# Memory attention and a four-expert feed-forward: the product of v_m and w1, by pairs of batches or by fours through device memory

## The chip, the cores and the metric

The kernel runs on one core of one Trainium2 chip. The metric is the device time of one execution in microseconds (us); three timed executions of the kernel before gave 1426.92, 1427.36 and 1427.86 us, median 1427.36 us. A separate execution was profiled.

## What is computed

An attention over 32 memory slots for each of 8 batches and 8 heads, and then a feed-forward of four experts over all 4608 rows. Cut to what matters:

```
a = softmax(phi, axis=2)                                   # (8, 8, 576, 32)
k_m = einsum('bhsm,bhsd->bhmd', a, k)
v_m = einsum('bhsm,bhsd->bhmd', a, v)                      # (8, 8, 32, 64)
attn = softmax(q @ k_m^T / 8)                              # (8, 8, 576, 32)
x = (attn @ v_m) laid out as (4608, 512)
for e in range(4):
    h = relu(x @ w1[e])                                    # (4608, 1024)
    out += p[:, e:e+1] * (h @ w2[e])
```

The kernel doesn't form x. It multiplies v_m of a batch with w1 first (256 rows, 8 heads of 32 slots, by 1024), and the attention weights with that product: h = relu(attn @ (v_m w1)).

## The kernel before

All values are fp32, and each large product is made as three TensorE matmuls on split operands: a value is held as a high part (a cast to fp32r) and a low part (value minus high part), and high*high, high*low and low*high are added in PSUM. ScalarE (ACT) makes the high part, VectorE (DVE) the low one.

The eight batches are worked through in four pairs (`k`), and in each pair the four experts (`e`). One pair and expert is a block of 32 steps: 16 for the even batch, 16 for the odd one (`odd`), each in two halves of 8 steps (`j`, one slice of 128 of the 1024 hidden columns). There are 512 steps. In a step, `first` (L415 to L417) multiplies attention weights `AT` with the product `vw` for the step after next (`AHEAD = 2`); ACT and DVE make `h` (and `hm`) of it (L427, L429); `second` (L445 to L447) multiplies `h` of this step with `w2` into PSUM, and after 8 steps DVE adds the result to `acc` (L460, L462).

Everything else is spread over the steps by tables: `plan` holds for each step the units that are written into the program ahead of the step's own matmuls. In each block:

- `unit_w2` (steps 20 to 27) and `unit_w1` (steps 24 to 30) split the next block's weights (ACT L118, DVE L119) from a staged load (`stage`, 512 KB each, five buffers, issued in order by SyncE, SP).
- `vw_unit` (steps 26 to 33) makes the next block's product of v_m and w1: for each half of w1 and each pair of heads three matmuls (L364 to L366, stationary `vt`, moving `w1`) into a tile `pv`. The stationary operand `vt` holds both batches of the pair, two heads of each on the diagonal, so one `pv` serves both; ACT and DVE split it into the two batches' `vw` tiles, 64 partitions at a time (L379, L380).
- The attention of the next pair's batches (softmax of phi, `unit_kv`, `kv_pick`, `write_vt`, scores and transposes) has step tables of its own (`UNITS_EVEN`, `UNITS_ODD`).

A scheduler then fixes each engine's order, with the place in the program as priority; each engine runs its queue in that order. Ahead of step 0 stands a part whose order is written by hand: batch 0's attention, its first products and the first two `first`. There `kv_pick` (L261, L265) and `write_vt` (L291) feed the scores and the first `pv`, and the chain reduce, add, reciprocal, multiply (L326 to L329) gives the attention weights, which PE transposes (L349) and DVE splits into `AT` (L356).

Of the kernel before, what the change touches and what calls it, by code (L numbers as in the profile page):

```python
# [68 lines left out]
def body(ctx: ExitStack, tc: tile.TileContext, qm, qt, kv, kvt, phi, prob, w1, w2, out):  # L70
    nc = tc.nc
    pool = lambda name, **k: ctx.enter_context(tc.tile_pool(name=name, bufs=1, **k))
    const, wp, work, att = pool("const"), pool("wp"), pool("work"), pool("att")
# [207 lines left out]
    def write_vt(b, a=slice(0, 2)):  # L281
        k, odd = b // 2, b % 2
        if ("vt", k) not in st:
            st["vt", k] = att.tile([P, NP, 2, P], F32R, name="vt", tag="vt", bufs=2)
        vt = st["vt", k].rearrange("p (a two) h c -> p a two h c", two=2)
        v = kvT[odd].rearrange("p w (a two) c -> p w a two c", two=2)
        for par in range(2):
            dst = vt[:, a, par ^ odd, :, 64 * par:64 * par + 64]
            src = v[:, 1, a, par, :]
            nc.scalar.copy(dst[:, :, 0, :], src)  # L290
            nc.vector.tensor_sub(dst[:, :, 1, :], src, dst[:, :, 0, :].bitcast(F32))  # L291
# [77 lines left out]
    def vw_out(ps, fh, hp, odds):  # L369
        g = hp // 2  # L370
        for odd in odds:
            if hp % 2 == 0:
                vw[odd, fh, g] = att.tile(
                    [P, 2, 512], F32R, name="vw", tag=f"vw{odd}", bufs=4 + odd
                )
            q = (hp % 2) ^ odd
            r = slice(64 * q, 64 * q + 64)
            t = vw[odd, fh, g]
# [289 lines left out]
```

## Time and profile before

| | before |
|---|---|
| median of three executions | 1427.36 us |
| profiled execution | 1428.84 us, of it span 1427.1 us |
| PE (TensorE) busy | 1412.3 us, 99% |
| DVE busy | 837.2 us, 59% |
| ACT busy | 620.2 us, 43% |
| loads and stores | 113.86 MB, 24.5% of the 16 DMA engines' span |

The span reaches from the first to the last instruction of the program; the profiled execution's own time is 1.74 us longer. A matmul's record is longer than its pitch, since matmuls are pipelined: one of 512 columns has a record of 0.39 us. What one costs where PE is never idle is therefore read from the starts of neighbours in the timeline, not from the mean of a group.

### The profile page before, as it was taken

Reading aid. Unit: us, or ns where it says so; the run is one execution under the profiler, and the core shown is the slowest. Engines: PE = TensorE matmul, PEld = TensorE weight load, DVE = VectorE, ACT = ScalarE, POOL = GpSimd, SP = SyncE. Lnnn points to the kernel's source line nnn. Section 1 sums busy time; section 2 is a strip of 40 time slices with the busy share of each in tenths; the row PEclk is TensorE's granted clock in tenths of the full one; section 3 lists DMA queues with packets and bytes.
Section 4 is the critical chain, followed back from the end, with each engine's and each line's share of the span. In section 5 each row is a group of like instructions: output and inputs, shape, how many; then the busy total and the mean of one; then the engine's idle time right before and its main releaser. Section 6 shows DMA issues by size and latency. Waiting matters only on the chain.

```text
span 1427.1 us, 20830 instructions
## 1 busy us (share of the span) xinstructions
PE 1412.3 (99%) x7808; PEld 1233.5 (86%) x7808; DVE 837.2 (59%) x1853; ACT 620.2 (43%) x1543; POOL 27.8 (2%) x27
## 2 busy tenths in 40 slices
PE   7999999999999999999999999999999999999998
PEld 6888888888888888888888888888888888888887
DVE  7876638666385654837547375573846446272722
ACT  6655426453263533635335362452625234161521
POOL 3300000000000000000000000000000000000000
PEclk8999999999999999999999999999999999999999
DMA  6632303323141120412214121140323103030001
GB/s 245 198 118 75 121 28 126 104 64 104 39 161 61 64 89 16 137 58 78 94 63 135 59 88 65 46 130 18 107 75 96 60 25 94 1 119 1 1 30 38
DMA packets 35957, 115.20 MB, mean 81 GB/s; under 512 B 3984, under 2 KB 5136, under 8 KB 35856
## 3 DMA queue, kind: packets, MB, share of 16 engines
q1 hardware_dynamic: 35856, 113.86, 24.5%
q8 instruction: 62, 1.02, 0.3%
q14 instruction: 39, 0.32, 0.1%
HBM read 104.41 MB, written 9.44 MB: 80 GB/s over the span
## 4 chain that ended last, share of the span: by engine, by line
PE 92%; DMA 2%; DVE 2%; ACT 2%; issue 1%; POOL 0%; SPq 0%; ACTq 0%
PE p L446 18%; PE p L447 18%; PE p L445 18%; PE p L415 9%; PE p L417 9%; PE p L416 9%; PE sc L304 2%; PE pv L366 2%; PE pv L364 2%; PE x L230 2%; PE pv L365 2%; DMA stage<-in_w 1%; PE tp L349 1%; PE kvp L249 1%; ACT w L118 0%
## 5 line engine op out<-in xcount | busy, mean ns | idle before, releaser
L446 PE MATMUL p<-w,h 128*128 128x512 f32 x1024 | 404.3, 395 | 0.0
L447 PE MATMUL p<-w,h 128*128 128x512 f32 x1024 | 402.8, 394 | 0.0
L445 PE MATMUL p<-w,h 128*128 128x512 f32 x1024 | 402.7, 393 | 0.0
L427 ACT ACTIVATE h<-p 128x256 fp32r<-128x256 f32 x512 | 195.2, 382 | 331.5 <-PE p L417 294.3
L429 DVE SCALAR_TENSOR_TENSOR h<-p,h 128x256 fp32r<-128x256 f32 x512 | 213.9, 418 | 206.3 <-ACT h L427 110.0
L415 PE MATMUL p<-AT,vw 128*128 128x256 f32 (+1 forms) x1024 | 308.2, 301 | 0.0
L417 PE MATMUL p<-AT,vw 128*128 128x256 f32 (+1 forms) x1024 | 304.3, 297 | 0.1
L416 PE MATMUL p<-AT,vw 128*128 128x256 f32 (+1 forms) x1024 | 303.6, 297 | 0.0
L447 PEld LDWEIGHTS p<-w,h 128*128 128x128 f32 x1024 | 192.4, 188 | 43.3 <-DVE nm L154 0.2
L119 DVE TENSOR_TENSOR w<-stage,w 128x512 fp32r<-128x512 f32 x259 | 175.9, 687 | 78.4 <-ACT w L118 77.1
L445 PEld LDWEIGHTS p<-w,h 128*128 128x128 f32 x1024 | 193.2, 189 | 23.3
L446 PEld LDWEIGHTS p<-w,h 128*128 128x128 f32 x1024 | 192.6, 188 | 22.0
L416 PEld LDWEIGHTS p<-AT,vw 128*128 128x128 f32 x1024 | 194.5, 190 | 19.5 <-DVE AT L356 0.3
L415 PEld LDWEIGHTS p<-AT,vw 128*128 128x128 f32 x1024 | 194.0, 189 | 19.1
L417 PEld LDWEIGHTS p<-AT,vw 128*128 128x128 f32 x1024 | 193.5, 189 | 0.7 <-DVE vw L380 0.6
L118 ACT CAST w<-stage 128x512 fp32r<-128x512 f32 x262 | 159.6, 620 | 79.1 <-DMA stage<-in_w 47.3
L380 DVE TENSOR_TENSOR vw<-pv,vw 64x512 fp32r<-64x512 f32 x254 | 172.1, 685 | 8.9 <-ACT vw L379 5.5
L429 DVE SCALAR_TENSOR_TENSOR hm<-p,hm 128x64 fp32r<-128x64 f32 x256 | 56.0, 219 | 201.9 <-ACT h L427 200.9
L379 ACT CAST vw<-pv 64x512 fp32r<-64x512 f32 x254 | 145.5, 580 | 58.5 <-DVE vw L380 42.6
L427 ACT ACTIVATE hm<-p 128x64 fp32r<-128x64 f32 x256 | 56.6, 221 | 227.9 <-PE p L417 227.9
L462 DVE SCALAR_TENSOR_TENSOR acc<-p,pt,acc 128x512 f32<-128x512 f32 x96 | 67.8, 741 | 2.6 <-PE p L447 2.6
L366 PE MATMUL pv<-w,vt 128*128 128x512 f32 x136 | 53.7, 395 | 0.0
(81 smaller groups left out, 1020.5 us busy)
## 6 DMA issues: line engine op xcount, KB each, us to landing
stage<-in_w SPq DMA_DIRECT2D x132, 512.0 KB, 3.8
stage<-in_kv SPq DMA_DIRECT2D x32, 512.0 KB, 4.1
stage<-in_qm SPq DMA_DIRECT2D x16, 512.0 KB, 3.7
out<-acc SPq DMA_DIRECT2D x32, 256.0 KB, 2.1
ph<-in_phi SPq DMA_DIRECT2D x16, 288.0 KB, 3.5
stage<-in_kvt SPq DMA_DIRECT2D x8, 512.0 KB, 3.8
stage<-in_qt SPq DMA_DIRECT2D x8, 128.0 KB, 3.2
out<-accm SPq DMA_DIRECT2D x4, 256.0 KB, 2.2
```

The source lines that it names most:

```text
L118: nc.scalar.copy(dst[:, 0, :], raw)
L119: eng.tensor_sub(dst[:, 1, :], raw, dst[:, 0, :].bitcast(F32))
L379: nc.scalar.copy(t[r, 0, :], ps[r])
L380: nc.vector.tensor_sub(t[r, 1, :], ps[r], t[r, 0, :].bitcast(F32))
L415: nc.tensor.matmul(ps, w[:, 0, f], at_t[:, g, 0, c], start=g == 0, stop=False)
L416: nc.tensor.matmul(ps, w[:, 0, f], at_t[:, g, 1, c], start=False, stop=False)
L417: nc.tensor.matmul(ps, w[:, 1, f], at_t[:, g, 0, c], start=False, stop=g == 1)
L427: nc.scalar.activation(t[:, 0, to], ps[:, at_], AF.Relu)
L429: nc.vector.scalar_tensor_tensor(t[:, 1, to], ps[:, at_], 0.0, t[:, 0, to].bitcast(F32), ALU.max, ALU.subtract)
L445: nc.tensor.matmul(po[t], x[:, 0, :], w[:, 0, :], start=j == 0, stop=False)
L446: nc.tensor.matmul(po[t], x[:, 0, :], w[:, 1, :], start=False, stop=False)
L447: nc.tensor.matmul(po[t], x[:, 1, :], w[:, 0, :], start=False, stop=j == NJ - 1)
```

## The change

- **Fours.** For some experts the product of v_m and w1 is made once for four batches (two pairs) and not once for each pair. `four` takes one head of w1 (64 rows, loaded twice into 128 partitions, input `w1d`), splits it, and multiplies with `vs`: 64 partitions of v's high part and 64 of its low part, four batches side by side in the 128 columns. Two matmuls give (high + low) * (w1 high + w1 low). `FOUR = (3, 0)`: batches 0 to 3 for expert 3 alone, batches 4 to 7 for all four experts. The other experts of batches 0 to 3 keep `vw_unit`.
- **Through device memory.** The 128x512 result is split into a tile `vst` of 128x2x512 (512 KB; ACT L466, DVE L467), which goes to device memory by one transfer (`to_memory`, L453), written in the program with the next `four`. For each block `load_vw` then loads a batch's rows: per batch and half of w1 eight transfers of 32 partitions, 128 KB each (L483), into the same `vw` tiles as before. All are issued by SP.
- **Where they stand.** In the blocks that make fours, one `four` a step in steps 8 to 23 (`FOUR_AT`), loads at steps 20, 25, 28 and 32 (`VW_LOAD_AT`); the blocks are the third of pair 0, the last of pair 1 and the first three of pair 2. Five other blocks (the third of pair 1, the last of pair 2, the first three of pair 3) have the loads alone, and no product of v_m and w1.
- **Attention.** Keys and values of batches 2 to 7 are made earlier, in tables of their own (`ATT`), since v of four batches must be there before the first `four`. The keys lie in four tiles `kT`, v apart in `v`. `kv_pick` has eight instructions for half as many elements each where it had four; `write_vs` and `v_hi` are added for every batch, `write_vt` stays for batches 0 to 3, in smaller pieces.
- **Buffers.** `stage` 5 to 4, `w2` 10 to 9, `kvs` (shared by `vst`) 2 to 3.

The diff, cut to its core:

```diff
-STAGE = 5
-KVS = 2
+STAGE = 4
+KVS = 3
 AHEAD = 2
+VW_LOAD_AT = ((20, 25), (28, 32))
+TURN = (0, 2, 1, 3)
+
+FOUR = (3, 0)
+
+FOUR_AT = ((8, 10, 12, 14), (16, 18, 20, 22))
...
-UNITS_EVEN = (0, 4, 6, 6, 7, 9, 10, 13, 16, 19, 22, 37, 42, 42, 46, 49, 49)
-UNITS_EVEN_0 = (29, 33, 36, 37, 37, 39, 40, 43, 46, 49, 50, 64, 69, 73, 73, 80, 81)
-UNITS_ODD = (63, 66, 68, 69, 69, 71, 72, 75, 78, 81, 84, 99, 104, 104, 109, 111, 112)
+
+
+PHI = 3
+KV_STEPS = (5, 5, 6, 8, 9, 12, 15, 18, 21)
+EVEN, ODD = (0, 4, 4, 8, 11, 11), (0, 5, 5, 10, 12, 13)
+ATT = {
+    2: (0, 27, (73, EVEN)), 3: (0, 49, (99, ODD)),
+    4: (PAIR, 2, (37, EVEN)), 5: (PAIR, 28, (99, ODD)),
+    6: (PAIR, 54, (PAIR + 37, EVEN)), 7: (PAIR, 80, (PAIR + 99, ODD)),
+}
...
-    kvT = [const.tile([P, 2, NP, 2 * M], F32, name=f"kvT{i}") for i in range(2)]
-    for t in kvT:
+    kT = [const.tile([P, NP, 2 * M], F32, name=f"kT{i}") for i in range(4)]
+    vts = [const.tile([P, NP, 2, P], F32R, name=f"vt{i}") for i in range(2)]
+    for t in [vts[0].bitcast(F32)] + kT + [vts[1].bitcast(F32)]:
         nc.gpsimd.memset(t, 0.0)
...
-                t = wp.tile([P, 2, DM], F32R, name="w2", tag="w2", bufs=NJ + 2)
+                t = wp.tile([P, 2, DM], F32R, name="w2", tag="w2", bufs=NJ + 1)
...
-        kvd = kvT[b % 2][:, :, 2 * g:2 * g + 2]
-        kvp = st["kvp", b, g].rearrange("p h w c -> p w h c")
-        for i in range(2):
-            r, m = slice(64 * i, 64 * i + 64), slice(M * i, M * i + M)
-            if i == 0:
-                nc.scalar.copy(kvd[r, :, :, m], kvp[r, :, :, m])
-            else:
-                nc.vector.tensor_copy(kvd[r, :, :, m], kvp[r, :, :, m])
-        for i in range(2):
-            r, m = slice(64 * i, 64 * i + 64), slice(M * i, M * i + M)
-            lo = slice(2 * M + M * i, 2 * M + M * i + M)
-            nc.vector.tensor_add(kvd[r, :, :, m], kvd[r, :, :, m], kvp[r, :, :, lo])
+        if g == 0:
+            st["v", b] = att.tile([P, NP, M], F32, name="v", tag="v", bufs=2)
+        for w in (1, 0):
+            for i in range(2):
+                r, m = slice(64 * i, 64 * i + 64), slice(M * i, M * i + M)
+                lo = slice(2 * M + M * i, 2 * M + M * i + M)
+                a = slice(2 * g, 2 * g + 2)
+                dst = st["v", b][r, a] if w else kT[b % 4][r, a, m]
+                src = st["kvp", b, g][r, :, w]
+                (nc.vector.tensor_copy if i else nc.scalar.copy)(dst, src[:, :, m])
+                nc.vector.tensor_add(dst, dst, src[:, :, lo])
...
+    def slot(b, h):
+        return h ^ TURN[b % 4]
+
+    def v_hi(b, gs=slice(0, 2)):
+
+        if ("vh", b) not in st:
+            st["vh", b] = att.tile([P, NP, M], F32R, name="vh", tag="vh")
+        split = lambda t: t.rearrange("p (g a) m -> p g a m", g=2)
+        v, vh = split(st["v", b]), split(st["vh", b])
+        if gs is not None:
+            nc.scalar.copy(vh[:, gs], v[:, gs])
+        return v, vh
+
+    def write_vt(b, gs=slice(0, 2)):
+
+        v, vh = v_hi(b, None)
+        vt = vts[b // 2].rearrange("p (g a) s c -> p g a s c", g=2)
+        for h in range(4):
+            q = slot(b, h)
+            r, rq = (slice(64 * (i % 2), 64 * (i % 2) + 64) for i in (h, q))
+            dst = vt[r, gs, h // 2, :, M * q:M * q + M]
+            x, hi = v[rq, gs, q // 2, :], vh[rq, gs, q // 2, :]
+            if r == rq:
+                nc.scalar.copy(dst[:, :, 0, :], x)
+                hi = dst[:, :, 0, :]
+            else:
+                nc.vector.tensor_copy(dst[:, :, 0, :], hi.bitcast(F32))
+            nc.vector.tensor_sub(dst[:, :, 1, :], x, hi.bitcast(F32))
+
+    def write_vs(b):
+
+        if b % 4 == 0:
+            st["vs", b // 4] = att.tile([P, 2, 4, P], F32R, name="vs", tag="vs")
+        vs, (v, vh) = st["vs", b // 4], v_hi(b, None)
+        for h in range(4):
+            q = slot(b, h)
+            rq, c = slice(64 * (q % 2), 64 * (q % 2) + 64), slice(M * q, M * q + M)
+            x, hi = v[rq, :, q // 2, :], vh[rq, :, q // 2, :]
+            if q % 2 == 0:
+                nc.scalar.copy(vs[:64, :, h, c], hi.bitcast(F32))
+            else:
+                nc.vector.tensor_copy(vs[:64, :, h, c], hi.bitcast(F32))
+            nc.vector.tensor_sub(vs[64:, :, h, c], x, hi.bitcast(F32))
...
+    vwd, done = {}, []
+
+    def to_memory():
+        for key, t in done:
+            vwd[key] = dram.tile([P, 2, 512], F32, name="vwd" + "".join(map(str, key)))
+            nc.sync.dma_start(vwd[key], t.bitcast(F32))
+        done.clear()
+
+    def four(n, e, fh, h, raw):
+
+        to_memory()
+        g, vs = h // 4, st["vs", n]
+        w = wp.tile([P, 2, 512], F32R, name="w1", tag="w1", bufs=4)
+        split(w, raw[:, h % 2, :], nc.vector)
+        ps = psum.tile([P, 512], F32, name="pv", tag="pm", bufs=4)
+        for a in range(2):
+            nc.tensor.matmul(ps, vs[:, g, h % 4, :], w[:, a, :], start=a == 0, stop=a == 1)
+        t = att.tile([P, 2, 512], F32R, name="vst", tag="kvs", bufs=KVS)
+        nc.scalar.copy(t[:, 0, :], ps)
+        nc.vector.tensor_sub(t[:, 1, :], ps, t[:, 0, :].bitcast(F32))
+        done.append(((n, e, fh, g, h % 4), t))
+
+    def units_four(n, e, fh, hp):
+        kept = []
+        def emit(raw):
+            kept.append(raw)
+            four(n, e, fh, 2 * hp, raw)
+        return (("w1d", e, fh, hp), emit), lambda: four(n, e, fh, 2 * hp + 1, kept[0])
+
+    def load_vw(k, e, odd, fh):
+        b = 2 * k + odd
+        for g in range(2):
+            t = vw_tile(k, e, odd, fh, g)
+            for h in range(4):
+                r = slice(M * slot(b, h), M * slot(b, h) + M)
+                nc.sync.dma_start(t[r].bitcast(F32), vwd[b // 4, e, fh, g, h][r])
...
+        def write():
+            v_hi(b)
+            if b < 4:
+                write_vt(b)
+            write_vs(b)
+        u += [write]
...
+                by_four = ne >= FOUR[nk // 2]
                 n = 0
                 for fh in range(2):
-                    for g in range(2):
+                    for hp in range(NP if by_four and nk % 2 == 0 else 0):
+                        for i, u in enumerate(units_four(nk // 2, ne, fh, hp)):
+                            at(s + FOUR_AT[fh][hp] + i, u)
+                    if by_four and nk % 2 == 0:
+                        at(s + FOUR_AT[fh][NP - 1] + 2, to_memory)
+                    for odd in range(2 if by_four else 0):
+                        at(s + VW_LOAD_AT[odd][fh], lambda a=(nk, ne, odd, fh): load_vw(*a))
+                    for g in range(0 if by_four else 2):
                         at(s + W1_AT[2 * fh + g], unit_w1(nk, ne, fh, g))
...
-        if k + 1 < NG:
-            b = 2 * k + 2
-            for bb, U in ((b, UNITS_EVEN_0 if k == 0 else UNITS_EVEN), (b + 1, UNITS_ODD)):
-                s0 = k * PAIR
-                at(s0 + U[0], lambda bb=bb: load_phi(bb))
-                at(s0 + U[1], lambda bb=bb: phi_chain(bb))
-                for n, u in enumerate(att_units(bb)):
-                    at(s0 + U[2 + n], u)
+    for b in range(2, B):
+        s0, kv_at, sc_at = ATT[b]
+        u = att_units(b)
+        at(s0 + kv_at, lambda b=b: load_phi(b))
+        at(s0 + kv_at + PHI, lambda b=b: phi_chain(b))
+        for d, x in zip(KV_STEPS, u[:9]):
+            at(s0 + kv_at + d, x)
+        for d, x in zip(sc_at[1], u[9:]):
+            at(s0 + sc_at[0] + d, x)
...
-        write_vt(1)
...
+    v_hi(0)
+    write_vs(0)
...
+        "w1d": c(
+            np.tile(moe_w1.reshape(E, NP, 2, D, 2, 512).transpose(0, 4, 1, 3, 2, 5), (1, 1, 1, 2, 1, 1))
+        ),
```

On PE, a step in the last eight of a block before (one `vw_unit`), and a step of a block with fours after; `vt` and `vs` are the stationary operands with v, `w` is split w1. Before:

```order
L447 MATMUL p_7353<-w_6546,h 128x512
L364 MATMUL pv<-w_7459,vt 128x512
L365 MATMUL pv<-w_7459,vt 128x512
L366 MATMUL pv<-w_7459,vt 128x512
L415 MATMUL p_7523<-AT,vw 128x256
```

After:

```order
L537 MATMUL p_8399<-w_7895,h 128x512
L464 MATMUL pv<-w_8437,vs 128x512 x2
L505 MATMUL p_8446<-AT,vw 128x320
L506 MATMUL p_8446<-AT,vw 128x320
L507 MATMUL p_8446<-AT,vw 128x320
```

Where three matmuls of 512 columns stood between two steps' own, two stand. In the whole program the first form goes from 136 units (408 matmuls) to 56 (168), and 80 of the second (160 matmuls) are new.

On DVE, in the part ahead of step 0, between the sum of the first softmax and the first split of `AT`. Before:

```order
L327 TENSOR_SCALAR z<-z 128x16
L328 RECIPROCAL z<-z 128x16
L329 TENSOR_TENSOR at<-at,z 128x512
L380 TENSOR_TENSOR vw<-pv,vw 64x512
L119 TENSOR_TENSOR w_420<-stage,w_420 128x512
L356 TENSOR_TENSOR AT<-tp,AT 128x2x256
```

After:

```order
L341 TENSOR_TENSOR vs<-v,vh 64x2x32
L377 TENSOR_SCALAR z<-z 128x16
L340 CAST vs<-vh 64x2x32
L341 TENSOR_TENSOR vs<-v,vh 64x2x32
L378 RECIPROCAL z<-z 128x16
L341 TENSOR_TENSOR vs<-v,vh 64x2x32
L379 TENSOR_TENSOR at<-at,z 128x512
L340 CAST vs<-vh 64x2x32
L435 TENSOR_TENSOR vw<-pv,vw 64x512
L341 TENSOR_TENSOR vs<-v,vh 64x2x32
L138 TENSOR_TENSOR w_451<-stage,w_451 128x512
L406 TENSOR_TENSOR AT<-tp,AT 128x2x256
```

Six small instructions that fill `vs` of batch 0 now stand in that chain, four of them ahead of the multiplication (L379) for which PE's transposes wait, two between it and the split of `AT` (L406).

On SP, from the start of pair 2's first block; `DMAHW` names the transfer whose landing frees the counter that is used again. Before, from the last two stores of pair 1 on:

```order
L464 DMA out<-acc 128x512 [waits DMAHW0_49,DVE_49]
L464 DMA out<-acc 128x512 [waits DMAHW1_49,DVE_49]
L104 DMA stage<-in_w 128x1024 [waits DMAHW3_49,DMAHW2_49,DVE_49]
L104 DMA stage<-in_w 128x1024 [waits DMAHW4_49,DVE_49,Activation_49]
L104 DMA stage<-in_w 128x1024 [waits DMAHW2_49,DVE_49]
L104 DMA stage<-in_w 128x1024 [waits DMAHW5_49,DMAHW4_49,DVE_49]
L146 DMA ph<-in_phi 128x576 [waits DMAHW6_49,PE_49]
L146 DMA ph<-in_phi 128x576 [waits DMAHW7_49]
L104 DMA stage<-in_w 128x1024 [waits DMAHW0_49,DVE_49]
```

After, in the same block where the fours' stores begin:

```order
L123 DMA stage<-in_w1d 128x1024 [waits DMAHW0_49,Activation_49]
L453 DMA vwd_8403<-vst 128x1024 [waits DMAHW1_49,DVE_49]
L123 DMA stage<-in_w1d 128x1024 [waits DMAHW2_49]
L453 DMA vwd_8435<-vst 128x1024 [waits DMAHW3_49,DVE_49]
L453 DMA vwd_8465<-vst 128x1024 [waits DMAHW4_49,DVE_49]
L123 DMA stage<-in_w1d 128x1024 [waits DMAHW5_49]
L453 DMA vwd_8497<-vst 128x1024 [waits DMAHW6_49,DVE_49]
L453 DMA vwd_8527<-vst 128x1024 [waits DMAHW7_49,DVE_49]
L123 DMA stage<-in_w 128x1024 [waits DMAHW0_49]
L453 DMA vwd_8559<-vst 128x1024 [waits DMAHW1_49,DVE_49]
```

Stores of `vst`, each waiting for the DVE instruction that ends it, now stand between the loads of w1.

## Rows read from the trace of the kernel before

**Rows 1.** The page's first part: the span, and busy time, share of the span and instructions of each engine.

```profile
span 1427.1 us, 20830 instructions
PE 1412.3 (99%) x7808; PEld 1233.5 (86%) x7808; DVE 837.2 (59%) x1853; ACT 620.2 (43%) x1543; POOL 27.8 (2%) x27
```

**Rows 2.** The page's second part: busy share in tenths of 40 equal slices, and the clock that TensorE was granted.

```profile
PE   7999999999999999999999999999999999999998
PEclk8999999999999999999999999999999999999999
```

**Rows 3.** Waits of PE over the whole span: who waited for whom, us in total, times, longest; the two longest.

```profile
PE x L230 <- DVE a L188: 2.7, 1, 2.7
PE tp L349 <- DVE at L329: 2.0, 1, 2.0
```

**Rows 4.** Busy time by stretches: us from the span's start, length, busy us and instructions of each engine, clock, share of the DMA engines, GB/s. The part ahead of step 0, then steps 0 to 511, then the last eight steps of a block in which no attention is made.

```profile
0.00:31.00 31.00, 22.30 (x127) 20.07 (x127) 22.54 (x45) 20.49 (x45) 14.11 (x17) 0.88 0.72 265
31.00:1423.00 1392.00, 1389.73 (x7684) 1213.42 (x7683) 813.58 (x1808) 599.68 (x1499) 13.72 (x10) 1.00 0.24 76
1163.00:1185.30 22.30, 22.30 (x122) 19.26 (x121) 19.17 (x34) 16.27 (x32) 0.00 (x0) 1.00 0.36 106
```

**Rows 5.** PE's timeline around one `vw_unit` in that last stretch: start us, length us.

```profile
1168.54 0.39 PE L447 MATMUL p<-w,h 128*128 128x512 f32 x1
1168.76 0.39 PE L364 MATMUL pv<-w,vt 128*128 128x512 f32 x1
1168.99 0.39 PE L365 MATMUL pv<-w,vt 128*128 128x512 f32 x1
1169.21 0.40 PE L366 MATMUL pv<-w,vt 128*128 128x512 f32 x1
1169.45 0.28 PE L415 MATMUL p<-AT,vw 128*128 128x256 f32 x1
```

**Rows 6.** Groups of instructions by line, over the whole span: shape, count | busy us, mean ns of one | idle time before them. PE's weight load for one matmul.

```profile
L447 PEld LDWEIGHTS p<-w,h 128*128 128x128 f32 x1024 | 192.4, 188 | 43.3 <-DVE nm L154 0.2
```

**Rows 7.** The same view: the product's split and the split of weights on DVE, the one split from PSUM over 128 partitions (DVE and ACT), and the smallest piece of `write_vt`.

```profile
L119 DVE TENSOR_TENSOR w<-stage,w 128x512 fp32r<-128x512 f32 x259 | 175.9, 687 | 78.4 <-ACT w L118 77.1
L380 DVE TENSOR_TENSOR vw<-pv,vw 64x512 fp32r<-64x512 f32 x254 | 172.1, 685 | 8.9 <-ACT vw L379 5.5
L356 DVE TENSOR_TENSOR AT<-tp,AT 128x512 fp32r<-128x512 f32 x16 | 11.1, 691 | 17.9 <-ACT AT L355 17.7
L291 DVE TENSOR_TENSOR vt<-kvT,vt 128x64 fp32r<-128x64 f32 x4 | 0.7, 223 | 0.3 <-ACT vt L290 0.3
...
L355 ACT CAST AT<-tp 128x512 fp32r<-128x512 f32 x16 | 9.4, 586 | 23.1 <-PE tp L349 16.5 <-PE p L417 6.6
```

**Rows 8.** The same view: what a batch's softmax of phi, its transposes, its tail and one `unit_kv` cost DVE (each stands there twice for a batch or unit).

```profile
L219 DVE TENSOR_TENSOR kvs<-stage,kvs 128x512 fp32r<-128x512 f32 x54 | 37.2, 722 | 8.7 <-ACT kvs L218 8.4
...
L151 DVE TENSOR_REDUCE nm<-ph 128x1 f32<-128x576 f32 x16 | 11.8, 742 | 3.6 <-DMA ph<-in_phi 3.6
...
L188 DVE TENSOR_TENSOR a<-tpa,a 128x512 fp32r<-128x512 f32 x16 | 10.7, 684 | 3.9 <-ACT a L187 3.9
...
L167 DVE TENSOR_SCALAR ph<-ph,zs 128x576 f32<-128x576 f32 x16 | 8.7, 541 | 0.5
L205 DVE TENSOR_TENSOR tl<-stage,tl 64x512 fp32r<-64x512 f32 x12 | 8.3, 689 | 0.4
```

**Rows 9.** DVE's timeline ahead of step 0: start us, length us, in brackets the idle time before and what ended it.

```profile
17.82 0.29 DVE L261 COPY kvT<-kvp 64x128 f32<-64x128 f32 x1 [0.91 <-ACT kvT L259]
18.15 0.60 DVE L265 TENSOR_TENSOR kvT<-kvT,kvp 64x128 f32<-64x128 f32 x2
19.06 0.37 DVE L291 TENSOR_TENSOR vt<-kvT,vt 128x64 fp32r<-128x64 f32 x2 [0.31 <-ACT vt L290]
20.69 0.29 DVE L261 COPY kvT<-kvp 64x128 f32<-64x128 f32 x1 [1.27 <-ACT kvT L259]
21.02 0.60 DVE L265 TENSOR_TENSOR kvT<-kvT,kvp 64x128 f32<-64x128 f32 x2
...
26.98 0.53 DVE L327 TENSOR_SCALAR z<-z 128x16 f32<-128x16 f32 x1
...
27.83 1.42 DVE L329 TENSOR_TENSOR at<-at,z 128x512 f32<-128x512 f32 x1
...
30.73 0.69 DVE L356 TENSOR_TENSOR AT<-tp,AT 128x512 fp32r<-128x512 f32 x1
```

**Rows 10.** PE's timeline at the end of the same part.

```profile
29.30 0.66 PE L349 MATMUL tp<-ident,at 128*128 128x128 f32 x4 [1.98 <-DVE at L329]
...
31.48 0.58 PE L416 MATMUL p<-AT,vw 128*128 128x256 f32 x1
```

**Rows 11.** DMA issues by line, over the whole span: count, KB each, median us from issue to landing.

```profile
stage<-in_w SPq DMA_DIRECT2D x132, 512.0 KB, 3.8
...
out<-acc SPq DMA_DIRECT2D x32, 256.0 KB, 2.1
```

**Rows 12.** The same view for the first 31 us.

```profile
stage<-in_w SPq DMA_DIRECT2D x7, 512.0 KB, 7.5
...
stage<-in_qm SPq DMA_DIRECT2D x1, 512.0 KB, 10.1
```

More of the change, by code (lines that the diff above doesn't have):

```diff
@@ L34 @@
 PSUM = bass.MemoryType.PSUM
+DRAM = bass.MemoryType.DRAM
 B, H, S, D, M = 8, 8, 576, 64, 32
@@ L69, in body @@
 @with_exitstack
-def body(ctx: ExitStack, tc: tile.TileContext, qm, qt, kv, kvt, phi, prob, w1, w2, out):
+def body(ctx: ExitStack, tc: tile.TileContext, qm, qt, kv, kvt, phi, prob, w1, w1d, w2, out):
     nc = tc.nc
@@ L73, in body @@
     const, wp, work, att = pool("const"), pool("wp"), pool("work"), pool("att")
+    dram = pool("dram", space=DRAM)
     psum = pool("psum", space=PSUM)
@@ L279, in unit_kv @@
         return ("kv", b, hp), emit
[L281 to L291, printed above, removed]
+    def slot(b, h):
[35 more added lines that the diff above has]
+            nc.vector.tensor_sub(vs[64:, :, h, c], x, hi.bitcast(F32))
     def tiles(t0):
@@ L297, in scores_mm @@
         nt, n = tiles(t0)
-        kvd = kvT[b % 2]
+        kvd = kT[b % 4]
         if hps[0] == 0:
@@ L304, in scores_mm @@
                 nc.tensor.matmul(
-                    sc[:n, i, hp, :], q[:, hp, i * P:i * P + n], kvd[:, 0, hp, :],
+                    sc[:n, i, hp, :], q[:, hp, i * P:i * P + n], kvd[:, hp, :],
                     start=True, stop=True,
@@ L361, in vw_mm @@
     def vw_mm(k, fh, hp, tag):
-        vt, w = st["vt", k], w1t[fh, hp]
+        vt, w = vts[k], w1t[fh, hp]
         ps = psum.tile([P, 512], F32, name="pv", tag=tag[0], bufs=tag[1])
@@ L367, in vw_mm, with vw_tile, vw_rows, vw_out @@
         return ps
-    def vw_out(ps, fh, hp, odds):
-        g = hp // 2
-        for odd in odds:
[L372 to L378, printed above, removed]
+    def vw_tile(*key):
+        if key not in vw:
+            odd = key[2]
+            vw[key] = att.tile([P, 2, 512], F32R, name="vw", tag=f"vw{odd}", bufs=4 + odd)
+        return vw[key]
+    def vw_rows(b, hp):
+        q = slot(b, 2 * (hp % 2)) // 2
+        return slice(64 * q, 64 * q + 64)
+    def vw_out(ps, k, e, fh, hp, odds):
+        for odd in odds:
+            t = vw_tile(k, e, odd, fh, hp // 2)
+            r = vw_rows(2 * k + odd, hp)
             nc.scalar.copy(t[r, 0, :], ps[r])
@@ L413, in first @@
         for g in range(2):
-            w = vw[odd, j // 4, g]
+            w = vw[k, e, odd, j // 4, g]
             nc.tensor.matmul(ps, w[:, 0, f], at_t[:, g, 0, c], start=g == 0, stop=False)
@@ L474, in att_units @@
         u += [unit_kv(b, hp) for hp in range(NP)]
-        u += [lambda: write_vt(b)]
+        def write():
[4 more added lines that the diff above has]
+        u += [write]
         u += [unit_scores(b, t0) for t0 in (0, 2, 4)]
@@ L607, in body @@
         for i in range(2):
-            t = wp.tile([P, 2, DM], F32R, name="w2", tag="w2", bufs=NJ + 2)
+            t = wp.tile([P, 2, DM], F32R, name="w2", tag="w2", bufs=NJ + 1)
             nc.scalar.copy(t[:, 0, :], raw["w2", 0, 0][:, i, :])
@@ L619, in body @@
         keep_warm(6)
-        vw_out(pv[1], 0, 1, (0,))
+        vw_out(pv[1], 0, 0, 0, 1, (0,))
         transposes(0, 0)
         keep_warm(4)
-        vw_out(pv[3], 0, 3, (0,))
+        vw_out(pv[3], 0, 0, 0, 3, (0,))
         for s in range(AHEAD):
@@ L641, in slots @@
     def slots(a):
-        return np.stack([a[b] if b % 2 == 0 else a[b][[2, 3, 0, 1, 6, 7, 4, 5]] for b in range(B)])
+        heads = lambda b: [i ^ TURN[b % 4] for i in range(H)]
+        return np.stack([a[b][heads(b)] for b in range(B)])
     q, k, v, phi = slots(q), slots(k), slots(v), slots(phi)
```

8 lines of the change are left out of this document (3 added, 5 removed).

## The prediction

> **What bounds the kernel now.** I read the page's first two parts, then PE's waits, then busy time by stretches, then single timelines. The first part says PE 99% of the span, DVE 59%, ACT 43% [rows 1]; the reader should not stop there, since a busy PE can still be a waiting one. So look at the slices: PE is at 9 tenths or more in all but the first and the last, and the granted clock is 8 tenths in the first slice and 9 or more (2.4 GHz) after it [rows 2]. PE's list of waits holds a few single waits, the longest 2.7 us and 2.0 us [rows 3], both ahead of step 0. The stretches say it plainly: from 31 to 1423 us PE is busy 1389.73 of 1392.00 us, while ahead of step 0 it is busy 22.30 of 31.00 us at a clock of 0.88 [rows 4]. Two things bound the time: in the 512 steps, the number of columns that PE streams; ahead of step 0, a chain through DVE, ACT and the first loads. A gain in the steps is a matmul less; a cost can come in at both.
>
> **PE's matmuls, the main term.** One `vw_unit` is three matmuls of 512 columns; the starts of the five rows around it are 0.22, 0.23, 0.22 and 0.24 us apart, so each takes 0.23 us of a PE that waits for nothing [rows 5]. Before, there are 136 units of three, 408 matmuls. After, 56 units stay (168 matmuls) and 80 `four` bring two each (160). 408 - 168 - 160 = 80 matmuls go: 80 * 0.231 = 18.5 us, with ends of 80 * 0.22 = 17.6 and 80 * 0.24 = 19.2 us. It isn't even: a block with fours streams 32 where it had 24, and pays 1.8 us; a block with loads alone streams none, and gets back 5.5 us; five of each, 5 * 3.7 = 18.5 us. Other matmuls keep their number and shape.
>
> In the trace the weight load of a matmul takes 188 ns, less than the 230 ns between matmuls of 512 columns, and lies beside the matmul before it [rows 5, 6]; so columns set the pitch. The Trainium skill ("TensorE: Matmul & The Clock Gate", section "Back-to-back issue gap") gives about 131 ns per matmul of 512 columns in a sustained stream of weight loads and matmuls; by that the 80 would be worth 10.5 us. This trace doesn't agree: 220 to 240 ns.
>
> **DVE and ACT in the steps, at nothing but with bounds.** The split of a `vw_unit` is two instructions of 64 partitions on each engine, 685 ns on DVE; that of a `four` is one of 128 partitions, by its nearest row 691 ns on DVE and 586 ns on ACT; each `four` also splits its weights, 687 ns on DVE [rows 7]. In a block with fours DVE has 16 * (687 + 691) = 22.0 us in 16 steps, where it had 8 * 687 + 16 * 685 = 16.5 us in eight: more in all, but 1.38 us a step in place of 2.06. What hides it: in the last eight steps of a block before, DVE is busy 19.17 of 22.30 us and PE never waits [rows 4], because `h` is wanted two steps after its `first`, 2 * 1392 / 512 = 5.4 us. That cover is thinnest where the tables now put a batch's keys and values into those last eight steps beside the old products: the second block of pair 0 (batch 3) and of pair 1 (batch 6). There come 2 * (742 + 541 + 684 + 689 + 722) ns = 6.8 us of DVE [rows 8]; 19.2 + 6.8 = 26.0 us against 22.3 us, 3.7 us too much. Bounds: 0 if the surplus drains into the lighter steps on both sides, 2 * 3.7 = 7.4 us if all of it reaches PE. No gain below nothing, since PE has no wait there to lose. I take 1.0 us, near the lower end, because the stretch at 86% cost nothing.
>
> **Ahead of step 0.** `kv_pick` and `write_vt` are cut into more, smaller instructions. Before, a half of the heads takes 0.29 + 0.60 us in `kv_pick` and 0.37 us in `write_vt` [rows 9]. After, it is six instructions and four; no row has their size, the nearest is 128x64 at 223 ns [rows 7]: 1.34 and 0.89 us, so 0.45 + 0.52 = 0.97 us more for each half. The first half has cover: DVE idles 0.91, 0.31 and 1.27 us in it [rows 9]. The second has none; DVE then runs almost without a gap up to the multiplication for which PE waits 1.98 us [rows 9, 10]. In this stretch the order puts six small instructions of `vs` for batch 0 as well, four ahead of the multiplication (L329 before), two ahead of the split of `AT`, for which PE's second `first` matmul starts at 31.48, just after the split's end at 31.42 [rows 9, 10]: 6 * 0.223 = 1.34 us. Sum 2.3 us. Lower end: the six alone, 1.3 us. Upper end: both halves exposed, 1.9 us, and the six at the 0.53 us that a tiny instruction took there (L327) [rows 9], 3.2 us: 5.1 us. A gain is excluded: what is taken out (`write_vt` of batch 1 at the start) isn't on this chain.
>
> With four `stage` buffers for five, the load of w2 for the second pair of slices and the query loads behind it start only when a buffer is read out. SP runs in order, so each pushes back those behind it. Bounds: 0, and one whole landing, 3.8 us [rows 11]. I take 0.6 us, near the lower end, since PE still has the first steps' matmuls to stream.
>
> **The transfers, at nothing, and what they cost if not.** 80 stores of 512 KB and 320 loads of 128 KB are 84 MB more than the 114 MB of before. A store holds one of three `vst` buffers. A `four` comes each step, so a buffer has three steps, 3 * (2.72 + 0.46) = 9.5 us, from one ACT copy to the next; it needs 0.59 + 0.69 us [rows 7] and a landing. A store of 256 KB lands in 2.1 us and a load of 512 KB in 3.8 us [rows 11]: 5.1 us by the longer, 4.4 us to spare. The wait that comes in stands on ACT, and behind it stand the copies of `h`. The loads wait on SP for the stores; those of the even batch are written at steps 20 and 25 and wanted at 30 and 34, nine steps or 24 us later, those of the odd batch have 18 steps. I take 0.
>
> **Sum.** -18.5 + 2.3 + 0.6 + 1.0 + 0 = -14.6 us. On the profiled execution, 1428.84 - 14.6 = 1414.2 us; that execution was 1.5 us above the median, so 1427.36 - 14.6 = 1412.8, 1413 us. All best ends give 1427.36 - 19.2 + 1.3 = 1409.5; all worst ends -17.6 + 5.1 + 3.8 + 7.4 = -1.3 us, 1426 us.
>
> **The rivals.** *Transfers too late (slower).* In the 16 steps with fours the queue carries 8.4 MB of stores, 4.2 MB of w1, and about 2 MB of other loads, in 16 * 3.2 = 51 us: 285 GB/s. The only stretch with such traffic, the first 31 us with 265 GB/s, kept the DMA engines 72% busy [rows 4], and there 512 KB took 7.5 us, at most 10.1 us [rows 12]. It decides at 9.5 - 1.3 = 8.2 us: beyond, ACT waits for a buffer once in three fours, PE's two steps of cover are used up, and the rest is paid. At 10.1 us that is 1.9 us * 80 / 3 = 51 us, 1464 us; at 9 us, 21 us and 1434 us. For it: the traffic. Against it: the queue of the first 31 us was filled with loads issued all at once, here one store a step. Chance 9 in 100.
>
> *The cover fails.* Start and surplus come near their upper ends: 5.1 + 2 + 5 = 12 us, net -6.5 us, 1421 us. For it: DVE's surplus in two places; against it, that nothing was lost at 86%. Chance 11. With still more of it, or part of the rival above, the change lands within 0.2%: 5.
>
> *A matmul taken out frees less than its pitch*: if weight loads set it, 80 * 0.188 = 15.0 us go [rows 6], net -11.1, 1416 us. Against it: matmuls of 256 and 512 columns would then have one pitch. Chance 3. By the Trainium skill's 131 ns on the same page and section, the net would be -6.6 us and 1421 us.
>
> That the fours don't replace the old products is excluded: the order holds 160 and 168 of them.
>
> **How the numbers follow.** The forecast, 1409 to 1419 us, has 72; 3 and 11 beside it are still faster; 5 within 0.2% (2.9 us, about what a measurement of this kernel can tell from no change); 9 slower. Faster 86, same 5, slower 9. 72 and 3 and about half of the 11 make 8 in 10: 1408 to 1422 us.
>
> **What would show it.** In the profile after: 160 matmuls of the fours, 0.23 us apart; the steps from the first `first` to the end 17 to 18 us shorter; that first `first` some 2 to 3 us later than before; no wait of PE over 2 us in the blocks with fours; about 198 MB moved. Wrong would be: ACT waiting for stores before its copies to `vst`; PE waiting for `h` or for a `vw` load; steps of the fours above 3.2 us.

## The result, and the profile after

The kernel after takes 1436.54 us (median of 4 runs, 1434.91 to 1437.17) against 1427.19 us before (4 runs, 1426.92 to 1427.86): ratio 1.0063, 95% interval 1.0046 to 1.0080. It is slower, where 1413 us was forecast. The profiled execution took 1435.91 us, with a span of 1433.9 us at a granted clock of 0.995.

The page's first parts answer to [rows 1]: PE's share fell by one point only, and 199 MB are moved.

```profile
PE 1404.4 (98%) x7728; PEld 1216.5 (85%) x7728; DVE 804.2 (56%) x1877; ACT 575.5 (40%) x1495; POOL 29.1 (2%) x31
...
DMA packets 62840, 199.12 MB, mean 139 GB/s; under 512 B 10384, under 2 KB 11536, under 8 KB 62736
```

PE's timeline around one `four` (start us, length us) shows the new product as forecast: two matmuls from 801.72, the next instruction 0.46 us later, so 0.23 us each, as in [rows 5].

```profile
801.72 0.62 PE L464 MATMUL pv<-w,vs 128*128 128x512 f32 x2
802.18 0.31 PE L505 MATMUL p<-AT,vw 128*128 128x320 f32 x1
```

PE's waits (us in total, times, longest) answer to [rows 3]. Each is short, but most pairs are new: PE now waits for splits of weights and of `vst`, and for `h`.

```profile
PE pv L464 <- DVE w L138: 3.2, 3, 1.2
PE p L535 <- ACT h L517: 2.6, 3, 1.4
PE x L249 <- DVE a L207: 2.4, 1, 2.4
PE p L505 <- DVE at L367: 2.4, 2, 1.6
...
PE p L505 <- DVE vst L467: 1.4, 2, 0.7
```

The issues of DMAs (count, KB each, median us from issue to landing) answer to [rows 11]. The stores land in 3.6 us.

```profile
vwd<-vst SPq DMA_DIRECT2D x80, 512.0 KB, 3.6
vw<-vwd SPq DMA_DIRECT2D x320, 128.0 KB, 4.3
stage<-in_w1d SPq DMA_DIRECT2D x40, 512.0 KB, 4.7
```

Short waits add up, so I made a balance from the starts of all PE rows: for each stretch of steps, its length less the sum of its matmuls' unhindered pitches (0.2315 us for 512 columns, 0.147 for 320, 0.119 for 256, 0.109 for 128, 0.060 for 64), less the same of the kernel before. A stretch starts with the first matmul behind the last `second` of the step before it. This is the time **lost** over before, in us, in one profiled execution of each kernel; the matmuls themselves, counted, give -18.5 (in e12 -14.8, in e2 0). The columns after the first belong to the experiments below (e8's is 1.8, 2.9, -1.1, 3.5, 0.1, 0.4).

| steps | after | e1 | e2 | e3 | e5 | e6 | e7 | e9 | e10 | e11 | e12 |
|---|---|---|---|---|---|---|---|---|---|---|---|
| to 31 | 3.3 | 10.8 | 1.5 | 2.2 | 5.6 | 2.6 | 3.4 | 2.3 | 3.6 | 1.7 | 1.8 |
| 32-95 | 2.8 | 8.6 | 2.1 | 4.1 | 2.4 | 2.7 | 2.4 | 6.7 | 3.7 | 2.8 | 0.2 |
| 96-159 | -0.8 | 0.7 | -1.1 | -1.1 | -1.1 | -1.1 | -1.1 | -1.1 | -1.1 | -1.1 | -1.1 |
| 160-255 | 4.8 | 12.4 | 9.2 | 3.2 | 5.2 | 4.6 | -0.5 | 11.8 | 6.1 | 0.1 | 3.3 |
| 256-383 | 14.4 | 11.7 | 0.8 | 0.1 | 13.2 | 16.4 | 0.1 | 17.6 | 0.0 | 0.0 | 0.1 |
| 384-511 | 0.4 | 0.4 | 0.7 | 0.4 | 0.4 | 0.4 | 0.4 | 0.4 | 0.4 | 0.4 | 0.4 |

After: -18.5 + 24.9 = 6.4 us, of the 6.8 by which the span grew. (The medians lie 9.35 us apart: the profiled execution before was 1.65 us above its median, the one after 0.63 us below.) Columns scatter: in e3's 4.1 and e10's 3.7 lies a single wait of PE at step 64, 1.94 and 1.59 us, that e7, with the same order of PE there, hasn't. So a difference under 2 us between two columns says little by itself.

Some of the loss is clock. From 998.5 to 1001.9 us, behind waits of 1.22, 0.71 and 0.59 us, TensorE was granted 1.2 GHz in place of 2.4 (0.50 in the row: start and end, length, busy time by engine, granted clock, share of the DMA engines, GB/s), and matmuls of 512 columns start 0.43 us apart in place of 0.23: about 1.5 of the 14.4 us that steps 256 to 383 lose.

```profile
998.50:1001.90 3.40, 3.29 (x8) 2.61 (x9) 1.77 (x4) 1.03 (x3) 0.00 (x0) 0.50 0.53 192
```

The largest part of the loss lies in steps 256 to 383. There, in the order of PE, the lead of `first` over `second` is lost: from 811.25 us `second(269)`, `(270)` and `(271)` stand back to back, `first(272)` only behind them. SP's timeline there (issues; one row can hold several):

```profile
787.60 0.37 SPq L123 DMA_DIRECT2D stage<-in_w1d  x1
798.25 0.34 SPq L453 DMA_DIRECT2D vwd<-vst  x1
798.64 0.42 SPq L123 DMA_DIRECT2D stage<-in_w1d  x1
800.98 3.05 SPq L453 DMA_DIRECT2D vwd<-vst  x2
804.08 0.42 SPq L123 DMA_DIRECT2D stage<-in_w1d  x1
818.15 3.26 SPq L453 DMA_DIRECT2D vwd<-vst  x2
```

SP stands from 788 to 798 us at a store whose product isn't made yet, with a load of weights behind it; so loads go out one at a time between stores. The store goes out at 798.25, just behind the end of the DVE instruction that completes its tile:

```profile
797.53 0.69 DVE L467 TENSOR_TENSOR vst<-pv,vst 128x512 fp32r<-128x512 f32 x1
```

On ACT, the copy to `vst` of a `four` whose matmuls began at 804.45 runs only at 812.86, in the order behind three steps' `h` and splits of weights; on DVE the accumulation, which waits for PE, stands ahead of the split for which PE then waits:

```profile
802.38 0.59 ACT L466 CAST vst<-pv 128x512 fp32r<-128x512 f32 x1 [1.23 <-PE pv L464]
...
811.83 1.14 ACT L137 CAST w<-stage 128x512 fp32r<-128x512 f32 x2
812.86 0.60 ACT L466 CAST vst<-pv 128x512 fp32r<-128x512 f32 x1
```

```profile
814.88 1.44 DVE L550 TENSOR_SCALAR acc<-p,pt 128x512 f32<-128x512 f32 x2 [2.35 <-PE p L537]
816.24 1.28 DVE L138 TENSOR_TENSOR w<-stage,w 128x512 fp32r<-128x512 f32 x2
```

Each engine here waits for one that waits in its own queue.

### The profile page after: what moved, and what is told of

Same layout as the page of the kernel before. It is cut to its first block, busy times and chain, and to the rows that moved or that the text cites. A ratio compares the mean times of both kernels' runs of the same rounds, so it can differ in the third digit from the quotient of the medians.

```text
span 1433.9 us, 21301 instructions
## 1 busy us (share of the span) xinstructions
PE 1404.4 (98%) x7728; PEld 1216.5 (85%) x7728; DVE 804.2 (56%) x1877; ACT 575.5 (40%) x1495; POOL 29.1 (2%) x31
## 4 chain that ended last, share of the span: by engine, by line
PE 55%; DVE 2%; ACT 0%; DMA 0%; issue 0%; DVEq 0%
PE p L537 11%; PE p L536 11%; PE p L535 11%; PE p L505 6%; PE p L507 6%; PE p L506 6%; PE pv L464 2%; PE sc L354 1%; PE x L249 0%; DMA stage<-in_kv 0%; DVE w L138 0%; PE tp L399 0%; DVE mx L364 0%; DVE kvs L238 0%; DVE acc L552 0%
## 5 line engine op out<-in xcount | busy, mean ns | idle before, releaser
L467 DVE TENSOR_TENSOR vst<-pv,vst 128x512 fp32r<-128x512 f32 x80 | 54.7, 688 | 35.1 <-ACT vst L466 34.2
L466 ACT CAST vst<-pv 128x512 fp32r<-128x512 f32 x80 | 46.7, 590 | 57.5 <-PE pv L464 48.7
L435 DVE TENSOR_TENSOR vw<-pv,vw 64x512 fp32r<-64x512 f32 x94 | 63.3, 685 | 5.9 <-ACT vw L434 4.8
```

The source lines that it names most:

```text
L435: nc.vector.tensor_sub(t[r, 1, :], ps[r], t[r, 0, :].bitcast(F32))
```

## The experiments

Medians; ratios are to the kernel before, with their 95% intervals.

**e1_lead**, in `second`:

```diff
-            nc.tensor.matmul(po[t], x[:, 0, :], w[:, 0, :], start=j == 0, stop=False)
+            i = nc.tensor.matmul(po[t], x[:, 0, :], w[:, 0, :], start=j == 0, stop=False)
+            tc.keep_in_program_order(i)
```

> The kernel after, with one edit: on PE every second(s) is queued behind first(s+2), so that the lead of two steps of the kernel before holds everywhere. In the trace of the kernel after the lead shrinks to one step or none at steps 62-64, 162, 192-195, 271-273, 291, 298, 335-337 and 355, and most stalls of PE lie there (17 us of stalls over 0.25 us more than before, 7.7 us of shorter ones). Theory (the fixed order lost the lead): about 12 of these 17 us come back, 1424 us, within 3 us. Rival (DVE and ACT have too much to do, or results are loaded too late): the waits only change their place, 1434 to 1438 us.

1453.95 us, 1.0194 (1.0178 to 1.0209): slower than either expected. My first theory fell: with the lead forced, PE waits for the work that was to fill its place (`kvp` for ACT's `xs`, 10.3 us in 14 waits).

```profile
PE kvp L268 <- ACT xs L260: 10.3, 14, 2.1
```

I took from it that a lost lead is the planner's answer to something late; this run alone doesn't show that.

**e2_no_fours**:

```diff
-FOUR = (3, 0)
+FOUR = (4, 4)
-KVS = 3
+KVS = 2
-    v_hi(0)
-    write_vs(0)
```
(and four `vt` tiles in place of two, `write_vt` for all batches, no `write_vs`)

> The keys and values of all batches at the places of the kernel after, but all products by the old units of three matmuls, and no transfer to device memory: what the moved attention and the longer prologue cost alone. The order of this kernel loses the lead at steps 62, 162, 192-195 and 221, but nowhere from 256 on. Theory (stalls lie where the lead is lost): 1427.2 plus about 2.5 us ahead of step 0 and 7 us in the blocks of steps 32, 160 and 192: 1437 us, within 3 us. Rival (the moved attention is harmless and all of it comes from the fours and their transfers): 1429 to 1430 us.

1443.83 us, 1.0120 (1.0105 to 1.0135): more than expected. The moved attention is a cost of its own, 2.1 us in steps 32 to 95 and 9.2 in 160 to 255 (about 1 of it at half clock, from 680.6 to 684.1 us), and 0.8 from 256 to 383. So nearly all that the kernel after loses there is due to the fours and their transfers.

**e3_stores_pool**:

```diff
-            nc.sync.dma_start(vwd[key], t.bitcast(F32))
+            nc.gpsimd.dma_start(vwd[key], t.bitcast(F32))
```

> The kernel after, with the 80 stores issued from GpSimd's queue in place of SP's. The order then keeps its lead everywhere from step 256 on (lost are 62, 64, 162, 192-195). Theory (one queue for stores and loads made the order drain the lead at 259 to 355): the 11 to 14 us that the blocks from 256 to 383 lose come back in most part, 1425 us, within 3 us. Rival (the engines' work there, or the transfers themselves): 1434 to 1438 us.

1421.23 us, 0.9964 (0.9955 to 0.9974): the theory, and a little more than it (its range began at 1422), and steps 256 to 383 lose 0.1 us in place of 14.4. SP's timeline in the same place:

```profile
778.76 3.27 SPq L483 DMA_DIRECT2D vw<-vwd  x7
782.12 1.32 SPq L123 DMA_DIRECT2D stage<-in_w1d  x3
```

Three loads of weights go out in one go, where the kernel after issues one and stands.

**e4_lead_twice** (e1, and in `to_memory` each store a second time):

```diff
+            twin = dram.tile([P, 2, 512], F32, name="twin" + "".join(map(str, key)))
+            nc.sync.dma_start(twin, t.bitcast(F32))
```

> As the run with the lead held on PE (e1_lead), and every result is stored a second time, to memory that nothing reads: 42 MB of stores more. Theory (the chip's transfers have slack): within 2 us of e1_lead. Rival (transfers bound the stages with fours): 8 us or more slower than e1_lead, with ACT's copies to vst waiting for transfers.

1521.14 us, 1.0662 (1.0645 to 1.0678): a miss, 67 us above e1; the rival's side, but not by its wait of ACT. PE waits for loads of `vw`, which have their place on SP among twice as many stores.

```profile
PE p L507 <- DMA vw<-vwd: 41.9, 5, 10.8
```

Queue and traffic are mixed in it; e9 has the stores on a queue of their own.

**e5_order_of_e3** and **e6_pool_old_order** hold the three engines' orders by edges between neighbours, for all that stands behind the part written by hand:

```diff
+        for a, b in zip(seq, seq[1:]):
+            tc.add_manual_dep(
+                own[b], own[a].name,
+                mybir.DependencyInfo(mybir.DependencyClass.NoSync, mybir.DependencyReason.DATA),
+                reason="hold_order",
+            )
```

> The kernel after, with its 80 stores on SP's queue as there, but with the instructions of PE, ACT and DVE held in exactly the order that they have in e3_stores_pool; only SP's queue differs from that run. Theory (the time lies in the fixed order of the compute engines, not in the queue of the transfers on the chip): as e3_stores_pool, 1421 us, within 3 us. Rival (SP's queue itself: a store that waits for DVE holds up the loads behind it): 1432 us or more, with PE, ACT or DVE waiting for loads.

> The other corner: stores on GpSimd's queue as in e3_stores_pool, but PE, ACT and DVE held in exactly the order of the kernel after. Theory (fixed order): as the kernel after, 1434 to 1438 us. Rival (queue): 1421 to 1424 us.

e5: 1433.68 us, 1.0053 (1.0038 to 1.0068): the rival. e6: 1441.24 us, 1.0109 (1.0092 to 1.0125): the theory, and 3 us over its range. So either alone is enough to lose the time: the old order with the stores off SP, or the new order with the stores on it. In steps 256 to 383 the order of the kernel after loses 14 to 16 us whatever the queue (about 1.5 and 3 of it at half clock); the order of e3 on SP's queue loses 13.2 us, by waits and by the clock behind them. (The table's e5 is an execution of 1436.43 us, 2.75 above the median, with 5.6 us lost up to step 31; its e6 one of 1436.66 us, 4.6 below.) In e5, SP and ACT in the same place:

```profile
778.62 5.16 SPq L483 DMA_DIRECT2D vw<-vwd  x8
...
784.90 3.71 SPq L483 DMA_DIRECT2D vw<-vwd  x8
788.74 0.35 SPq L123 DMA_DIRECT2D stage<-in_w1d  x1
800.13 0.34 SPq L453 DMA_DIRECT2D vwd<-vst  x1
...
802.87 3.05 SPq L453 DMA_DIRECT2D vwd<-vst  x2
...
806.44 0.77 SPq L123 DMA_DIRECT2D stage<-in_w  x1
```

```profile
813.38 0.62 ACT L137 CAST w<-stage 128x512 fp32r<-128x512 f32 x1 [7.62 <-DMA stage<-in_w]
813.90 0.58 ACT L466 CAST vst<-pv 128x512 fp32r<-128x512 f32 x1
```

A load of weights issued at 806.44, behind three stores (in e3 it goes out at 799.83), makes ACT wait 7.62 us; behind that wait stand the copy to `vst` and the next `h`, and PE waits 3.44 us for the PSUM buffer `pv`, and 4.37 us for another in the block of step 320. Behind both waits TensorE was granted 1.2 GHz, and nearly half of these 10.8 us of matmuls is lost too (the rows: start and end, length, busy time, clock 0.50): about 8 of the 13.2 us are waits, about 5 are clock.

```profile
815.38 1.22 PE L464 MATMUL pv<-w,vs 128*128 128x512 f32 x2 [3.44 <-DVE vst L467]
...
994.21 1.22 PE L464 MATMUL pv<-w,vs 128*128 128x512 f32 x2 [4.37 <-DVE vst L467]
```

```profile
815.38:821.41 6.03, 6.03 (x16) 5.07 (x17) 4.33 (x11) 2.90 (x9) 0.00 (x0) 0.50 0.77 279
994.21:998.97 4.76, 4.76 (x14) 4.08 (x14) 4.33 (x11) 2.91 (x9) 0.00 (x0) 0.50 0.69 276
```

In the blocks of steps 288 and 352, e5 loses nothing, the kernel after 3.7 and 2.1 us and e6 4.0 and 2.1: there the order alone costs.

**e7_kv_apart** (on e3):

```diff
-    4: (PAIR, 2, (37, EVEN)), 5: (PAIR, 28, (99, ODD)),
-    6: (PAIR, 54, (PAIR + 37, EVEN)), 7: (PAIR, 80, (PAIR + 99, ODD)),
+    4: (PAIR, 2, (37, EVEN)), 5: (PAIR, 32, (99, ODD)),
+    6: (PAIR, 62, (PAIR + 37, EVEN)), 7: (PAIR, 80, (PAIR + 99, ODD)),
```

> As e3_stores_pool, with the keys and values of batch 5 four steps later and those of batch 6 eight steps later, so that they don't lie on the eight steps of the old products (154 to 161 and 186 to 193). The order then keeps its lead at 162 and 192 to 195. In e3_stores_pool the blocks of steps 160 and 192 lose 1.0 and 2.2 us. Theory (DVE's surplus where keys and values meet the old products): 2 to 3 us less than e3_stores_pool, 1418.5 us. Rival (keys and values cost this wherever they stand): within 1 us of e3_stores_pool.

1417.51 us, 0.9936 (0.9921 to 0.9951). Steps 160 to 255 go from 3.2 us lost to 0.5 us gained: the theory.

**e8_vs_later** (on e3):

```diff
-    v_hi(0)
-    write_vs(0)
+    at(22, lambda: (v_hi(0), write_vs(0)))
-        for w in (1, 0):
+        for w in (1, 0) if b else (0, 1):
```
(and `write_vt` and `write_vs` fitted to it)

> As e3_stores_pool, with the six DVE and ACT instructions of vs for batch 0 moved from ahead of step 0 to step 22, and the keys of batch 0 picked ahead of its values. Theory (small instructions on the chain ahead of step 0): the first step starts 1.3 to 2.3 us earlier, 1419.5 us. Rival (that chain's length comes from what else moved): within 0.5 us of e3_stores_pool.

1419.42 us, 0.9956 (0.9942 to 0.9971). From the first row of the scores' matmuls to the first of `first` it is 12.1 us before, 14.1 after, 14.0 in e3 and 14.2 here, where the scores come earlier; `first` itself starts at 31.90 in place of 32.09 us. In e2, which has no `vs` at all, it is 14.0 too. The second matmul of `first` comes 0.53 us earlier (32.74 for 33.27), but the scores too begin 0.41 us earlier. The six instructions were not the cost there: a miss. That the time is the theory's is luck: in the profiled executions most of what e8 gains over e3 lies in steps 32 to 95 (2.9 lost for 4.1), where e3 has its single wait, and the two intervals overlap.

**e9_pool_twice** (e3, and each store a second time from GpSimd's queue):

> As e3_stores_pool, and every result is stored a second time from the same queue, to memory that nothing reads: 42 MB more, with the same order of PE. Theory (the transfers themselves have slack; a queue's order costs, not the traffic): within 2.5 us of e3_stores_pool, 1421 us. Rival (the traffic of stores and loads is what costs): 8 us or more slower, with ACT's copies to vst waiting for stores to land.

1451.25 us, 1.0164 (1.0149 to 1.0179): a miss; the rival, with its wait. Landings (median us) and ACT's wait:

```profile
vwd<-vst POOLq DMA_DIRECT2D x80, 512.0 KB, 6.8
twin<-vst POOLq DMA_DIRECT2D x80, 512.0 KB, 8.1
```

```profile
ACT vst L468 <- DMA twin<-vst: 102.4, 45, 4.8
```

Now the three `vst` buffers come free too late, and ACT waits. The slack of the transfers is real but finite: one store in each step fits, two don't.

**e10_loads_pool**, in `load_vw`:

```diff
-                nc.sync.dma_start(t[r].bitcast(F32), vwd[b // 4, e, fh, g, h][r])
+                nc.gpsimd.dma_start(t[r].bitcast(F32), vwd[b // 4, e, fh, g, h][r])
```

> The kernel after with the stores left on SP's queue and the 320 loads of vw moved to GpSimd's, so that on SP only loads of weights stand behind the stores; PE's order is that of e3_stores_pool. Theory (a store that waits for DVE holds up the weights' loads behind it): those loads still go out late and the blocks of steps 256 and 320 lose 5 to 6 us each as in e5_order_of_e3, 1431 us or more. Rival (it was the vw loads, 16 in a row, that held up the weights' loads): 1420 to 1423 us.

1425.94 us, 0.9992 (0.9983 to 1.0002): no different from the kernel before, and between the two expectations; the mechanism is the rival's. Nothing is lost from 256 to 383, though the stores still stand on SP: without the `vw` loads ahead of them, the weights' loads are out before the first store is reached.

```profile
771.92 10.65 SPq L123 DMA_DIRECT2D stage<-in_w1d  x5
```

It is both kinds in one queue that costs, loads that wait for a buffer or a landing and stores that wait for a product; either one moved away is enough. What makes it slower than e3 all the same lies before step 256 (1.4 us up to step 31 and 2.9 in steps 160 to 255). Of the 2.9, one wait is 2.67 us: PE at 599.50 us for ACT's split of `kvs`, and ACT 2.73 us for that load. Why it came late was not followed.

**e11_together** (the edits of e3, e7 and e8):

> The edits of e3_stores_pool, e7_kv_apart and e8_vs_later in one kernel. Theory (three separate costs): 1415.5 to 1417.5 us, a little under e7_kv_apart; left over are about 2 us ahead of step 0 and 2 us in the blocks of steps 32 and 64. Rival (they were one cost): as e3_stores_pool, 1420 us or more.

1415.62 us, 0.9915 (0.9900 to 0.9930): the theory, and the fastest of all, 11.9 us under the kernel before in the same series.

**e12_batch3_later** (on e11):

```diff
-FOUR = (3, 0)
+FOUR = (4, 0)
-    2: (0, 27, (73, EVEN)), 3: (0, 49, (99, ODD)),
+    2: (0, 29, (73, EVEN)), 3: (0, 66, (99, ODD)),
```

> As e11_together, but expert 3 of batches 0 to 3 goes back to the old products, so that the keys and values of batch 3 need not be done by step 72; they move from step 49 to 66, away from the old products of steps 58 to 65 (those of batch 2 from 27 to 29). That brings 16 matmuls back, 3.7 us. In e11_together the blocks of steps 32 and 64 lose 2.0 and 0.8 us more than before. Theory (DVE's surplus where keys and values meet the old products): these 2.8 us mostly come back, net 1 to 1.5 us above e11_together, 1416.8 us. Rival (that loss has another cause): 3.7 us above, 1419.3 us.

1419.42 us, 0.9949 (0.9936 to 0.9963): the rival's number, but not its mechanism. Steps 32 to 95 lose 0.2 us in place of 2.8, as the theory has it (steps 32 to 63, which have no fours in either kernel, go from 2.0 lost to 0.4 gained); but the eight old products that come back in steps 218 to 225 now meet the keys and values of batch 7 (213 to 229), and the block of step 192 loses 3.0 us.

## Why the prediction was wrong

- **PE's main term, -18.5 us: right.** The balance takes its -18.5 from the count, so it is no test; but the pitch of the fours is 0.23 us, so the rival at 0.188 is out, and a block with loads alone (steps 384 to 479) fell from 81.07 to 75.63 us, 5.4 against the 5.5 forecast.
- **The transfers, "at nothing": this step failed, by 14.4 us.** (About 1.5 of it is TensorE's half clock behind the waits.) I looked at a buffer's time and a landing (3.6 us against a bound of 8.2) and at when `vw` is wanted; both hold, and ACT waited for a store once, 0.6 us. I didn't ask what stands behind a waiting store or load on SP: the weights' loads. For the `stage` buffers the prediction says it ("SP runs in order, so each pushes back those behind it"), and the order on record ahead of it shows stores that wait for DVE between the loads of w1; I didn't put the two together. With the loads late, PE, ACT and DVE either wait (e5) or are ordered by the planner as if they did (the kernel after, e6). e3 and e10 take it away with the same transfers. The rival "transfers too late" had the sign, not the mechanism: the longest landing of a store is 7.4 us, so its 1434 us at 9 us is near by luck. In e9, where the later of two landings has a median of 8.1 us, it does decide.
- **DVE and ACT's surplus, +1.0 us (0 to 7.4): the right mechanism, the wrong size.** Steps 32 to 255 lose 2.8 - 0.8 + 4.8 = 6.8 us. That it is the meeting of keys and values with the old products, e7 shows for steps 160 to 255 and e12 for 32 to 63. I named batches 3 and 6; batch 5, which e7 also moves, meets them too, in steps 159 to 161. I chose the low end because a stretch at 86% had cost nothing; here most of the surplus did not drain into the lighter steps. e2 shows that this part alone, with the old products in all blocks, costs 2.1 - 1.1 + 9.2 = 10.2 us.
- **Ahead of step 0, +2.3 us (1.3 to 5.1): right in size, partly wrong in cause.** PE's waits, as in [rows 10]: `first` starts at 33.06 for 30.95 us, 2.1 later, and its second matmul at 34.24 for 31.48. The six instructions of `vs` are not it (e8, e2); what is left are the smaller pieces of `kv_pick` and `write_vt`, which was only argued.

```profile
31.73 0.66 PE L399 MATMUL tp<-ident,at 128*128 128x128 f32 x4 [0.87 <-DVE at L379]
...
34.24 0.39 PE L506 MATMUL p<-AT,vw 128*128 128x256 f32 x1 [0.79 <-DVE AT L406]
```

- **The `stage` buffers, +0.6 us: not shown, at most half of it.** Steps 2 to 31 lose 1.5 us of the 3.3 in the table's first row. But e2, with the same four `stage` and nine `w2` buffers, loses 0.3 us there. The rest is there in the runs with fours (nearly 1 us of it in steps 4 and 5, in e3, e8 and e12 too), and its cause is open.
- *The cover fails* described steps 32 to 255 well, but I gave it 5 us in all. With 6.8 there, 14.4 from queue and order, and 3.3 ahead of step 32, the gain is used up.

The Trainium skill ("DMA: Bandwidth & Descriptors", section "Issuing engines are not separate DMA queues") says that issuing from several engines saves only the time to issue. Of bandwidth no run here speaks against it; of time, e3 does: 80 issues moved to another engine gave 15 us, since what is saved is not the time of issuing but that of standing behind another's wait.

What stays open: why the planner's order loses time in the blocks of steps 288 and 352, where the chip (e5) needs no such order; its estimates are not in a trace. No run has the fours with five `stage` buffers, so how much of the 14.4 us a load issued further ahead would have hidden isn't known either.

## What to carry to other kernels

Before adding transfers to a queue, write down for each what it waits for, and what stands behind it; if they wait for different engines, try them in different queues. Bound not only how long a transfer takes but when it can be issued. And where a planner fixes the order, look for places where a lead of steps shrinks in it: such an order cost its time here even with the stores off the queue (e6). What helped was to take the lateness away and plan again (e3), not to force the lead (e1).
